# Linear attention with a GELU feed-forward on one core: weights loaded as fp32 pieces over two hardware queues in place of casting loads on GpSimd's queue

## The chip, the cores and the metric

The kernel runs on 1 core of one Trainium2 chip. The metric is the device time of one execution in microseconds, as a median of runs. The core has five engines: TensorE (PE, matmuls), VectorE (DVE), ScalarE (ACT), GpSimd (POOL) and SyncE (SP, here only for issuing DMAs). DMAs can be issued from SyncE's, ScalarE's and GpSimd's queues.

## What is computed

Linear attention with a decay per head (4 batches, 8 heads, 768 positions, head size 64), and on its output a feed-forward layer with the tanh form of GELU (512 to 2048 to 512 columns, 3072 rows, fp32 in and out):

```
for t in range(S):
    state = gamma[None, :, None, None] * state + np.einsum('bhd,bhe->bhde', k[:, :, t], v[:, :, t])
    y[:, :, t] = scale * np.einsum('bhd,bhde->bhe', q[:, :, t], state)
...
x = np.ascontiguousarray(attn_out.transpose(0, 2, 1, 3)).reshape(B * S, H * D)
h = x @ w_in
g = 0.5 * h * (1.0 + np.tanh(c * (h + 0.044715 * h * h * h)))
return (g @ w_out).astype(np.float32)
```

## The kernel before, in words

The 768 positions are cut into six chunks c of 128, and each chunk has the four batches b. What is done is a list of small steps, written out by hand in one string, `ORDER`. A word such as `PREP:q,0,2,P@1` calls the function `PREP` with chunk 0, batch 2 and engine P (A is ScalarE, V VectorE, P GpSimd, S SyncE); the numbers behind `@` name the buffers that the new tiles take. Every engine runs its own steps in the order of the list, and waits for what they need. So the list sets the order on each engine and in each DMA queue.

The steps of a chunk are these. `L` loads the rows of q, k or v of one batch as fp32, 256 KB, into one of 13 row buffers (class `r32`, slots 0 to 12). `PREP` converts them to fp16, and for some scales them by the decay. `T` with `ET`, or `DT` (a transposing DMA, from chunk 2 on), turns q and k. `A` and `EA` make the masked products of q and k, `SS` and `ES` the state, `YP` and `YI` the output of attention, and `EY` or `EP` bring it to SBUF as x, the input of the feed-forward layer.

The feed-forward layer has four blocks j of w_in (512 columns each) and of w_out (512 rows each). In most places its products are made by a scheme with seven products where eight would be plain: `M1` (seven for a chunk and a block) and `M2` (seven for the second product), with sums of weights made beforehand (`WI`, `WO`) and sums of inputs (`SX`, `SG`); `CP` and `D1` bring the results together, `G` is GELU. `HB` and `GB` are the plain form for one block and one batch of chunk 0: 16 matmuls with 128 columns against 4 matmuls with 256 columns in each `M1`. `O0` is the plain second product of chunk 0. `CO`, `D2` and `ST` (`ST0` for chunk 0) finish and store.

In the kernel before, block 1 of chunk 0 goes by `HB`, the other three by `M1`. The weights come by `LWI` (two DMAs for each block of w_in, one for each half of the partitions) and `LWO` (one for each block of w_out). These are issued on GpSimd and convert from fp32 to fp16 on the way; 23 of the 72 `L` are issued on GpSimd too. `SPIN` keeps TensorE running on zeros at the start. `HOLD` is a DMA of two fp16 numbers from a block of weights to a scratch tile, five of them on SyncE's queue; since it reads the weights, what follows it on SyncE's queue waits for them.

Of the kernel before, what the change touches and what calls it, by code (L numbers as in the profile page):

```python
# [31 lines left out]
GB:1,2,0@7 HB:1,1@5 ES:0,0,A GB:1,2,1@8 GB:1,0,1@9 PREP:q,1,2,V@2 PREP:k,1,2,V M1:0,3,3 HB:1,3@7 L:k,2,2,P@3
CP:0,3,12,A@1 GB:1,1,0 GB:1,1,1 T:1,1@6 L:q,2,1,P@4 ET:1,1,A@4 L:k,2,0,P@5 M1:0,3,7 T:1,3@0 L:v,2,0,P@12
T:1,2@3 D1:0,3,22 D1:0,3,12 O0:1,0@5 ET:1,3,A@5 ET:1,2,V@6 D1:0,2,22 M1:0,3,4 GB:1,3,1 L:q,2,0,P@0 T:1,0@6
WI:2,4,V GB:1,3,0 G:0,3,21@10 A:1,2@2,0 ET:1,0,A@0 EA:1,2,0@0 A:1,1@3,7 EA:1,1,1@1 O0:0,0@4 G:0,2,22@11 O0:1,1
A:1,3@6,2 EA:1,2,1 PREP:v,1,3,A@5 EA:1,1,0 A:1,0@7,0 M1:0,2,4 O0:0,1 PREP:v,1,1,A@6 G:0,2,21@12 EA:1,3,0@2
EA:1,0,1@3 EA:1,0,0 HOLD:1,2 YP:1,0@3,1 YP:1,1@6,0 PREP:v,1,0,A@7 YI:1,2 SS:1,2@7 L:v,2,3,P@9 EA:1,3,1 YI:1,0
L:q,2,2,S@11 WI:1,1,V WO:1,1,V G:0,3,11@13 YI:1,1 YI:1,3 EP:1,0,0,A@1 EP:1,0,1,V EP:1,1,0,A L:v,3,2,S@10
SS:1,1@2 SS:1,3 SS:1,0 G:0,3,12@14 O0:1,2 EP:1,1,1,A WO:2,1,V ES:1,1,V M1:1,0,1@3 M1:1,3,1@1 M1:1,1,2@6
G:0,3,22@15 CP:1,3,11,A@0 M1:1,1,1@0 SX:1,1,V@4 SX:1,3,V@5 CP:1,1,11,A@3 CP:1,0,11,A@1 WO:2,2,V SX:1,2,P@0  # L40
WI:1,3,V M1:1,3,2@7 O0:0,2 PREP:k,2,3,P@0 D1:1,3,11 O0:0,3 M1:1,1,5@7 G:1,3,11@16 ES:1,0,V EO:0,V@0 M1:1,3,5@2
PREP:k,2,1,A@2 M1:1,3,6 M1:1,0,2@4 CP:1,3,22,A@2 D1:1,1,11 WO:0,1,P G:1,1,11@17 PREP:q,2,3,P SX:1,4,P@1 O0:1,3
DT:2,3@1 CP:1,1,22,V@0 WO:3,1,P D1:1,0,11 PREP:k,2,2,A@3 L:v,2,1,S@6 M1:1,0,6 O0:2,0@6 CP:1,3,12,V@3
PREP:q,2,2,P PREP:v,2,2,P@0 M1:1,0,5@4 PREP:k,2,0,A@4 G:1,0,11@18 M1:1,3,7 M1:1,3,3 PREP:q,2,1,A CP:1,0,12,A@1
WI:1,2,V O0:2,1 PREP:q,2,0,P DT:2,1@2 DT:2,2@3 D1:1,3,22 LD:S D1:1,3,12 M1:1,1,6 EO:1,A@1 DT:2,0@0 HOLD:1,3
M1:1,1,3 L:v,3,3,S@1 WO:3,2,P G:1,3,22@19 CP:1,1,12,A@2 M1:1,0,7 WI:1,4,P G:1,3,12@20 M1:1,3,4 D1:1,1,12
G:1,3,21@21 A:2,3@2,5 M1:1,1,7 M1:1,2,5@7 O0:2,2 M1:1,2,1@1 EA:2,3,1@0 CP:1,0,22,A@3 PREP:v,2,1,P@3 D1:1,0,22
D1:1,1,22 WO:1,2,P G:1,1,12@22 G:1,1,22@23 EA:2,3,0 M1:1,0,3 L:k,3,0,S@2 M1:1,0,4 D1:1,0,12 O0:2,3
CP:1,2,22,V@2 CP:1,2,11,A@0 L:k,3,2,S@8 L:v,3,0,S@3 G:1,0,21@24 M1:1,1,4 M1:1,2,6 L:q,3,3,S@11 A:2,1@5,2
G:1,1,21@25 PREP:v,3,2,P@2 A:2,2@4,3 L:q,4,1,S@7 EO:2,V@2 EA:2,1,0@3 EA:2,2,1@1 G:1,0,22@26 A:2,0@0,6  # L50
CP:1,2,12,A@3 G:1,0,12@27 PREP:v,2,0,P@1 WO:0,2,P EA:2,0,0@2 L:q,3,2,S@5 PREP:v,2,3,P@4 M1:1,2,3 O0:3,0@5
O0:3,1 EA:2,0,1 L:q,3,0,S@4 M1:1,2,7 PREP:k,3,0,A@1 EA:2,1,1 YP:2,0@3,0 EA:2,2,0 L:k,3,3,S@0 L:k,5,1,S@6
YP:2,1@6,2 D1:1,2,12 YI:2,0 SG:1,1,1,P@28 L:q,3,1,S@10 PREP:v,3,3,P@6 L:q,4,2,S@12 SG:1,3,1,P@29 YI:2,1 YI:2,2
HOLD:0,0 YI:2,3 EP:2,0,1,V@0 SS:2,0@4 SS:2,3@7 D1:1,2,22 SS:2,2 EP:2,0,0,V SS:2,1 SG:1,1,2,P@30 ES:2,1,V
PREP:k,3,2,A@4 L:k,3,1,S@9 O0:3,2 G:1,2,22@31 M1:1,2,4 M1:1,2,2@0 EP:2,1,1,V O0:3,3 M1:2,0,1@3 D1:1,2,11
WO:0,3,P HOLD:0,3 WO:3,3,P ST0:2,S PREP:q,3,2,P L:v,3,1,S@2 PREP:q,3,3,A@0 M2:1,1,0,0@7 EP:2,1,0,V
# [10 lines left out]
M1:2,1,6 G:2,3,22@8 D1:2,1,11 PREP:v,3,1,P@5 G:2,3,12@11 A:3,0@5,3 A:3,2@2,0 PREP:v,3,0,P@7 L:k,4,1,S@9
SG:2,0,3,P@12 SG:1,1,3,P@10 CP:2,1,12,A@0 M1:2,1,3 M2:1,3,0,1 M2:1,6,0,0 WO:3,4,V EA:3,2,0@2 M1:2,2,1@2
M2:1,6,0,1 M2:1,3,1,0 M1:2,1,7 CO:1,12,A@2 M2:1,3,1,1 SG:1,3,3,P@15 EA:3,0,0@3 D1:2,1,12 EA:3,0,1 EA:3,2,1
D1:2,1,22 A:3,3@5,1 A:3,1@3,0 M1:2,1,4 L:q,4,3,S@0 G:2,1,21@24 EA:3,3,0@1 EA:3,3,1 EA:3,1,1@0 EA:3,1,0  # L70
L:v,5,2,S@12 CP:2,2,11,A@2 M2:1,7,1,0 M2:1,7,1,1 L:k,4,2,S@2 M2:1,7,0,0 PREP:v,4,0,P@1 D2:1,12, ST0:0,S
# [620 lines left out]
```

## Time and profile before

| what | value |
| --- | --- |
| median of 3 runs | 200.41 us (200.15 to 200.44) |
| the profiled execution's own time | 200.09 us |
| its span, first to last instruction | 198.3 us |
| mean granted TensorE clock | 0.98 |
| PE busy | 183.0 us (92%) |
| VectorE, ScalarE, GpSimd busy | 160.0, 119.3, 139.1 us |
| read from HBM, written | 27.63 MB, 6.29 MB |

The span leaves out what lies around the program's instructions, here 1.8 us. All times of the parts are from the one profiled execution. A busy share is an average over the whole span; which engine or transfer holds the others up differs from stage to stage. In rows of instructions, the numbers ahead are the start and the length in us, or the busy time and the mean in ns; `SPq` or `ACTq` is the sequencer of that engine when it issues a DMA.

### The profile page before, as it was taken

To read this page: it belongs to the slowest core of one execution; us is meant where nothing else is said; L and a number is where in the kernel's file an instruction comes from. 1 tells how busy PE (TensorE), PEld (TensorE's weight loads), DVE (VectorE), ACT (ScalarE), POOL (GpSimd) and SP (SyncE) were. 2 spreads that over 40 slices of the span, in tenths; PEclk is the share of its full clock that TensorE was granted. 3 is DMA by queue.
4 is the path that set the end of the run, shared out by engine and by line. 5 is a ranking of instruction groups with operands and counts; after the bars stand their busy time and mean duration, and the time that the engine had idled before them with its cause. 6 is when DMAs were issued, how large, how long until landed. Compare 5 with 4: busy or idle time off the path is not lost.

```text
span 198.3 us, 5294 instructions
## 1 busy us (share of the span) xinstructions
PE 183.0 (92%) x2111; PEld 149.0 (75%) x2111; DVE 160.0 (81%) x294; ACT 119.3 (60%) x219; POOL 139.1 (70%) x143
## 2 busy tenths in 40 slices
...
DMA  6999999999989999999999995260200201301453
GB/s 144 288 239 243 203 334 234 295 239 333 270 195 235 214 211 258 213 212 216 244 226 190 209 178 155 53 150 27 94 0 0 86 23 58 106 0 56 141 201 136
DMA packets 80540, 34.26 MB, mean 173 GB/s; under 512 B 69060, under 2 KB 78404, under 8 KB 80516
## 3 DMA queue, kind: packets, MB, share of 16 engines
q1 hardware_dynamic: 66164, 19.35, 44.4%
...
q10 hardware_dynamic: 8224, 4.36, 7.6%
...
HBM read 27.63 MB, written 6.29 MB: 171 GB/s over the span
## 4 chain that ended last, share of the span: by engine, by line
PE 65%; DMA 19%; POOL 6%; DVE 4%; issue 2%; ACT 1%; ACTq 0%; SPq 0%; POOLq 0%; DVEq 0%
PE bank L219 65%; DMA w_in<-in_moe_w_in_dram 9%; DMA r<-in_q_dram 6%; DMA qkT<-qk 2%; DVE g L216 2%; DMA r<-in_v_dram 2%; POOL sx L216 2%; POOL t_out L216 1%; POOL qk L216 1%; POOL v L216 1%; DVE h L216 1%; DVE w_out L216 1%; POOL g L216 1%; POOL w_in L262 0%; POOL qk L213 0%
## 5 line engine op out<-in xcount | busy, mean ns | idle before, releaser
L219 PEld LDWEIGHTS <-g 128*128 128x128 f16 x624 | 60.4, 98 | 11.8 <-PE bank L338 0.3
L216 POOL TENSOR_TENSOR g<-g 128x512 f16<-128x512 f16 x46 | 54.5, 1204 | 17.9 <-DVE g L216 7.2
L219 PE MATMUL bank<-w_out,g 128*128 128x256 f16 (+1 forms) x384 | 60.4, 290 | 0.2 <-DMA w_out<-in_moe_w_out_dram 0.2
L216 DVE TENSOR_TENSOR h<-bank,h 128x512 f32<-128x512 f32 x69 | 46.0, 682 | 8.8 <-PE bank L219 4.4
L442 ACT ACTIVATE g<-h 128x512 f16<-128x512 f32 x69 | 42.7, 634 | 15.4 <-DVE h L216 15.0
L219 PEld LDWEIGHTS <-w_in 128*128 128x128 f16 x432 | 39.2, 98 | 6.2 <-issue 0.8
L211 ACT COPY h<-bank 128x512 f32<-128x512 f32 x57 | 32.7, 588 | 13.0 <-PE bank L219 12.6
L219 PEld LDWEIGHTS <-t_in 128*128 128x128 f16 x276 | 26.4, 98 | 9.9 <-issue 4.3
L219 PE MATMUL bank<-t_out,g 128*128 128x256 f16 x240 | 33.4, 273 | 0.0
L216 DVE TENSOR_TENSOR a<-bank,mask 128x512 f16<-128x512 f32 x48 | 30.0, 680 | 3.5 <-PE bank L219 3.4
L219 PE MATMUL bank<-x,w_in 128*128 128x256 f16 (+1 forms) x248 | 29.7, 259 | 0.4 <-DMA w_in<-in_moe_w_in_dram 0.2
L219 PE MATMUL bank<-sx,t_in 128*128 128x256 f16 x184 | 26.5, 273 | 2.3 <-ACT g L442 1.2
L219 PE MATMUL bank<-sx,w_in 128*128 128x256 f16 x184 | 26.7, 273 | 0.0
L216 DVE TENSOR_TENSOR g<-g 128x512 f16<-128x512 f16 x34 | 22.1, 669 | 3.1 <-ACT g L442 2.1
L442 ACT ACTIVATE g<-bank 128x512 f16<-128x512 f32 (+1 forms) x31 | 16.5, 549 | 8.4 <-PE bank L219 5.8
L211 ACT COPY o<-bank 128x512 f32<-128x512 f32 (+1 forms) x19 | 9.7, 516 | 18.2 <-PE bank L219 18.2
L216 POOL TENSOR_TENSOR v<-r,cst 128x512 f16<-128x512 f32 x16 | 16.9, 1061 | 4.0 <-DMA r<-in_v_dram 4.0
L216 DVE TENSOR_TENSOR o<-bank,o 128x512 f32<-128x512 f32 (+1 forms) x18 | 10.6, 595 | 8.9 <-PE bank L219 8.7
L211 ACT CAST qk<-r 128x512 f16<-128x512 f32 x20 | 12.1, 620 | 6.2 <-PE bank L219 2.2
L219 PE MATMUL bank<-x,t_in 128*128 128x256 f16 x92 | 13.8, 273 | 1.9 <-DVE h L216 1.9
L216 DVE TENSOR_TENSOR qk<-r,cst 128x512 f16<-128x512 f32 x13 | 9.2, 744 | 6.5 <-DMA cst<-rr_cst 4.1
L211 ACT COPY qkT<-bank 128x1024 f16<-128x1024 f16 x7 | 6.9, 1013 | 8.0 <-PE bank L338 8.0
...
## 6 DMA issues: line engine op xcount, KB each, us to landing
r<-in_v_dram SPq DMA_DIRECT2D x15, 256.0 KB, 4.8
r<-in_q_dram SPq DMA_DIRECT2D x15, 256.0 KB, 4.2
r<-in_k_dram SPq DMA_DIRECT2D x14, 256.0 KB, 4.6
out_dram<-o ACTq DMA_DIRECT2D x11, 256.0 KB, 3.8
r<-in_v_dram POOLq DMA_DIRECT2D x9, 256.0 KB, 8.3
out_dram<-o SPq DMA_DIRECT2D x9, 256.0 KB, 2.3
w_in<-in_moe_w_in_dram POOLq DMA_DIRECT2D x8, 256.0 KB, 9.6
r<-in_k_dram POOLq DMA_DIRECT2D x8, 256.0 KB, 8.6
```

Of the source, the lines that this page charges most:

```text
L211: nc.scalar.copy(out=out, in_=in_)
L216: EN[e].tensor_tensor(out=out, in0=in0, in1=in1, op=op)
L219: nc.tensor.matmul(out=out, lhsT=lhsT, rhs=rhs, start=start, stop=stop, skip_group_check=True)
L442: nc.scalar.activation(out=out, in_=in_, func=AF.Gelu_apprx_tanh, scale=1.0)
```

## The change

The weights no longer come by converting DMAs from GpSimd. Each block of w_in and of w_out is loaded in four pieces of 128 rows and 512 columns as fp32 (for w_in the 128 rows are two runs of 64, 256 rows apart) (`WLI`, `WLO`, 256 KB each, 32 in all) into the row buffers that `L` uses, over SyncE's queue (26 pieces) and ScalarE's (6). A piece is then converted into its place in the fp16 block by `CWLI` or `CWLO`, 14 of them on ScalarE and 18 on GpSimd. All 72 `L` go over SyncE's (33) and ScalarE's (39) queues. The five `HOLD` are gone. Block 0 of chunk 0 now goes by `HB` too, so four `HB` and eight `GB` take the place of seven `M1`, three `CP`, three `D1` and four `G`. `ORDER` is written anew as a whole; some steps change their engine (`SG` on GpSimd 46 to 52, `PREP` on GpSimd 34 to 42, `CP` on VectorE 12 to 19). The new functions:

```diff
+    def WLI(j, kc, e):
+
+        t = new("r32", ("wi32", j, kc), [128, 512], F32)
+        src = moe_w_in.rearrange("(u k p) n -> u p k n", u=2, p=64)[:, :, kc, j * 512:(j + 1) * 512]
+        EN[e].dma_start(out=t, in_=src)
+
+    def WLO(j, kc, e):
+        t = new("r32", ("wo32", j, kc), [128, d_model], F32)
+        fc = 4 * j + kc
+        EN[e].dma_start(out=t, in_=moe_w_out[fc * 128:(fc + 1) * 128])
+
+    def CWLI(j, kc, e):
+        copy_on(e, w_in[j][:, kc], tiles["wi32", j, kc])
+
+    def CWLO(j, kc, e):
+        copy_on(e, w_out[j][:, kc], tiles["wo32", j, kc])
```

The beginning of the old and of the new order, up to where the first products of w_out begin in the new one:

```diff
-L:k,0,2,A@0 L:q,0,2,A@1 ZERO L:k,0,0,S@2 SPIN:11@0 LI:A L:q,0,3,A@3 LC:S TABLE PREP:k,0,0,V@0 L:k,0,3,A@4
-L:q,0,1,A@5 L:v,0,1,S@6 PREP:q,0,2,P@1 LWI:0 PREP:k,0,2,V L:v,0,3,P@7 MASK L:k,0,1,S@8 L:q,0,0,S@9
-PREP:q,0,3,V@2 T:0,2@1 ET:0,2,A@0 A:0,2@2,3 L:v,0,0,P@10 PREP:k,0,3,V LWI:2 L:v,0,2,S@11 T:0,3@4 PREP:q,0,0,V
-ET:0,3,A@1 PREP:k,0,1,P@3 EA:0,2,1@0 A:0,3@5,6 T:0,0@7 EA:0,2,0 ET:0,0,A@2 PREP:q,0,1,V T:0,1@0 LWI:3
-A:0,0@1,4 PREP:v,0,2,P@0 EA:0,3,0@1 EA:0,3,1 EA:0,0,0@2 EA:0,0,1 ET:0,1,A@3 LWI:1 SS:0,2@3 A:0,1@2,7
-EA:0,1,0@3 PREP:v,0,0,P@1 PREP:v,0,1,A@2 PREP:v,0,3,A@3 YI:0,2@5 SS:0,1@6 L:k,1,1,P@12 EA:0,1,1 EY:0,2,A@0
-L:q,1,3,S@2 YI:0,3@1 L:q,1,1,P@1 YI:0,0@4 WI:0,1,V L:q,1,2,P@0 WI:0,2,V SS:0,3 YI:0,1@0 EY:0,3,A SX:0,1,V@0
-EY:0,0,A EY:0,1,A L:k,1,0,P@3 SS:0,0 WI:0,3,V M1:0,0,5@2 M1:0,0,1@7 WI:0,4,V SX:0,2,V@1 SX:0,3,V@2
-CP:0,0,11,A@0 L:k,1,3,P@4 SX:0,4,V@3 L:k,1,2,P@9 M1:0,0,2@5 M1:0,2,1@1 LWO:0 M1:0,0,6 WI:2,1,V CP:0,0,22,A@1
-CP:0,2,11,A@2 D1:0,0,11 M1:0,2,2@4 WI:2,3,V M1:0,2,5@0 M1:0,0,3 CP:0,0,12,A@3 L:q,1,0,P@8 LWO:1 WI:2,2,V
-L:v,1,2,P@5 D1:0,2,11 G:0,0,11@0 CP:0,2,22,A@0 D1:0,0,12 M1:0,0,7 M1:0,2,6 G:0,2,11@1 ES:0,1,A L:v,1,3,P@11
-G:0,0,12@2 D1:0,0,22 L:v,1,1,P@10 L:v,1,0,P@6 M1:0,2,3 M1:0,3,2@5 WI:3,1,V CP:0,2,12,A@2 M1:0,0,4 M1:0,3,1@4
-PREP:q,1,3,V@4 WI:3,3,V LWO:2 PREP:q,1,0,P@1 LWO:3 D1:0,2,12 L:v,2,2,P@7 WI:3,2,V CP:0,3,11,A@3 M1:0,3,5@2
-L:k,2,1,P@2 G:0,2,12@3 PREP:q,1,1,V@3 D1:0,3,11 L:q,2,3,P@8 WI:3,4,V M1:0,2,7 G:0,0,21@4 HB:1,0@3 PREP:k,1,0,V
...
+WLI:1,3,A@0 ZERO L:k,0,2,S@1 SPIN:11@0 LC:S L:q,0,3,S@2 L:k,0,1,A@3 PREP:k,0,1,V@0 L:k,0,3,S@4 MASK
+L:q,0,1,A@5 PREP:q,0,1,V LI:A PREP:k,0,3,V@1 L:q,0,2,A@6 L:k,0,0,S@7 PREP:k,0,2,V@2 L:v,0,3,A@8 L:q,0,0,A@9
+T:0,1@1 L:v,0,1,A@10 WLI:0,3,A@11 PREP:q,0,3,P TABLE T:0,3@2 L:v,0,2,S@12 PREP:q,0,2,V CWLI:1,3,P ET:0,3,V@0
+L:k,1,1,S@3 WLI:2,2,A@5 T:0,2@3 ET:0,2,V@1 PREP:v,0,3,P@0 PREP:q,0,0,V@3 A:0,2@4,5 PREP:k,0,0,P ET:0,1,A@2
+A:0,3@6,7 T:0,0@0 EA:0,2,1@0 L:v,0,0,S@4 WLI:0,2,S@1 EA:0,3,0@1 A:0,1@2,3 WLI:2,1,A@2 EA:0,3,1 ET:0,0,A@3
+PREP:v,0,2,A@1 WLI:0,0,S@6 CWLI:2,2,P YI:0,3@1 PREP:v,0,1,P@2 PREP:v,0,0,P@3 EY:0,3,A@0 A:0,0@5,6 EA:0,1,0@2
+EA:0,2,0 PREP:k,1,1,P@4 EA:0,1,1 CWLI:2,1,A SS:0,3@7 WLI:0,1,S@0 CWLI:0,2,A WLI:2,0,S@8 YI:0,2@0 EA:0,0,1@3
+WLI:2,3,S@9 SS:0,2 YI:0,1@1 EA:0,0,0 YI:0,0@2 WLI:3,0,S@7 CWLI:0,1,P SS:0,0@4 CWLI:2,0,P CWLI:0,3,A CWLI:0,0,A
+WLI:3,1,S@12 EY:0,1,A EY:0,0,V EY:0,2,V SS:0,1 WI:2,1,V HB:0,3@3 WLI:1,2,S@5 WLI:3,3,S@10 ES:0,1,A CWLI:2,3,A
+WLI:3,2,S@4 SX:0,1,V@0 HB:0,1@6 CWLI:3,0,A GB:0,3,1@0 WI:0,1,V L:k,1,0,A@3 GB:0,3,0@1 M1:0,2,1@5 L:q,1,0,A@2
+WLI:1,1,S@1 ES:0,0,A WI:2,2,V CWLI:3,1,P M1:0,2,5@1 HB:0,2@2 M1:0,2,2@0 SX:0,2,V@1 CP:0,2,11,V@0 M1:0,3,1@7
+WI:3,1,V WLI:1,0,S@0 HB:0,0@3 CWLI:3,3,P L:k,1,2,S@8 GB:0,2,0 SX:0,4,V@2 CWLI:1,0,P CWLI:3,2,A GB:0,1,0@2
+L:q,1,2,S@11 CP:0,2,22,V@1 CWLI:1,1,P GB:0,2,1 L:q,1,1,S@6 CP:0,3,11,A@2 L:v,1,0,A@9 M1:0,3,5@4 CWLI:1,2,A
+SX:0,3,V@3 WI:2,3,V M1:0,3,2@2 L:q,1,3,S@7 WI:3,3,V PREP:q,1,2,P@1 M1:0,2,6 PREP:q,1,1,P WI:3,2,V L:k,2,2,A@12
+D1:0,2,11 WI:2,4,P M1:0,2,3 D1:0,3,11 L:k,1,3,S@10 G:0,2,11@3 WI:3,4,V CP:0,2,12,A@3 PREP:q,1,3,P@2 G:0,3,11@4
+GB:0,1,1@5 HB:1,0@0 L:v,1,2,A@0 PREP:k,1,2,V L:v,1,3,S@4 WI:1,1,V HB:1,1@2 PREP:k,1,0,V@3 PREP:q,1,0,V
+M1:0,3,6 CP:0,3,22,A@0 HB:1,3@6 M1:0,2,7 GB:0,0,1 GB:1,1,1@6 PREP:k,1,3,P M1:0,3,3 WLO:0,3,S@1 PREP:v,1,0,P@4
+L:v,1,1,A@5 D1:0,2,12 GB:1,0,0@7 GB:1,0,1 T:1,2@1 WLO:0,1,S@11 WLO:0,2,S@6 WLO:1,0,S@7 GB:1,1,0 CP:0,3,12,V@2
+M1:0,3,7 GB:0,0,0 ET:1,2,A@4 D1:0,2,22 PREP:v,1,1,P@5 WLO:0,0,S@8 T:1,1@0 T:1,0@2 A:1,2@3,1 GB:1,3,1@8
+D1:0,3,12 D1:0,3,22 ET:1,1,V@5 PREP:v,1,2,P@6 ET:1,0,A@6 EA:1,2,1@1 WLO:1,3,S@3 M1:0,2,4 M1:0,3,4 G:0,2,21@9
+PREP:v,1,3,P@7 A:1,1@4,0 G:0,3,12@10 EA:1,2,0 G:0,3,21@11 A:1,0@2,1 T:1,3@5 EA:1,1,0@0 EA:1,0,1@2 EA:1,0,0
+HB:1,2@3 ET:1,3,A@1 GB:1,3,0@12 YP:1,0@7,4 EA:1,1,1 WLO:1,1,S@2 A:1,3@1,2 CWLO:0,1,P EA:1,3,0@3 YI:1,0 YI:1,1
+G:0,2,12@13 YP:1,1@5,6 L:q,2,1,A@10 WLO:2,1,S@9 SS:1,1@0 SS:1,0 YI:1,2 EA:1,3,1 CWLO:0,3,P EP:1,0,1,A@1
+ES:1,0,V EP:1,0,0,A SS:1,3@1 SS:1,2 G:0,2,22@14 YI:1,3 WLO:2,0,S@5 M1:1,0,2@2 M1:1,3,1@4 EP:1,1,1,A CWLO:0,2,P
+WLO:1,2,S@0 ES:1,1,V GB:1,2,0 M1:1,1,1@0 M1:1,0,1@7 EP:1,1,0,A CP:1,0,11,A@2 WLO:3,2,S@4 PREP:k,2,2,P@0
+CWLO:0,0,P WI:0,2,V L:q,2,0,A@11 SX:1,1,V@4 M1:1,3,2@6 SX:1,3,V@5 CWLO:2,1,P G:0,3,22@15 CP:1,3,11,A@3
+O0:0,0@1 WLO:2,2,S@1 D1:1,0,11 GB:1,2,1 O0:2,0@5 CP:1,1,11,V@1 CWLO:1,1,A M1:1,1,2@2 D1:1,3,11 SX:1,2,P@0
+CWLO:1,2,A CWLO:2,0,A L:q,2,2,S@6 M1:1,3,5@3 CWLO:1,0,P WLO:2,3,A@12 CWLO:1,3,P G:1,0,11@16 SX:1,4,P@1
+M1:1,0,6 D1:1,1,11 L:k,2,1,A@8 M1:1,3,6 G:1,3,11@17 WI:0,4,V M1:1,0,5@6 O0:1,0@2 WI:1,2,V PREP:q,2,1,P@4
...
```

More of the change, by code (lines that the diff above doesn't have):

```diff
@@ L32 @@
[L32 to L56, printed above, removed]
@@ L67 @@
[L67 to L71, printed above, removed]
@@ L92 @@
-SG:2,3,4,V@14 M2:2,5,0,0@6 G:3,3,22@13 HOLD:1,1 M1:3,2,5@5 CP:3,2,12,A@2 EP:4,1,0,V SG:3,3,1,P@24 M1:4,1,1@4
-ES:4,0,V G:3,3,12@28 ST0:3,A CP:3,2,22,A@3 M2:2,7,0,0 SG:3,1,2,P@9 PREP:q,5,3,A@1 M2:2,5,1,0 M2:2,7,1,0
-M1:3,2,3 SG:2,2,3,P@36 M2:2,5,1,1 M1:4,1,2@0 M1:3,2,7 M1:4,0,1@1 PREP:k,5,0,A D1:3,2,12 M1:3,2,2@2 M2:2,5,0,1
-SX:4,1,V@0 D1:3,2,22 M1:4,1,5@5 CP:4,1,11,V@0 SX:4,2,P@4 M1:4,1,6 G:3,2,12@25 D1:4,1,11 L:v,5,3,S@9 D1:3,2,11
-M2:2,7,1,1 G:3,2,22@4 SX:4,4,P@3 CP:4,1,22,V@2 M1:4,0,2@0 CO:2,22,A@4 SX:4,3,P@1 DT:5,0@0 PREP:q,5,2,P@3
@@ new lines @@
+G:1,3,22@19 PREP:k,2,1,P WO:3,1,V D1:1,3,12 L:v,2,0,A@1 PREP:q,2,0,P@3 G:1,3,12@20 D1:1,0,12 M1:1,1,5@3
+CP:1,1,12,V@2 PREP:q,2,2,A M1:1,3,4 CWLO:3,1,A M1:1,2,1@6 M1:1,1,7 D1:1,0,22 CWLO:3,3,P O0:1,2 G:1,3,21@21
+M1:1,0,4 WO:1,2,P WI:1,4,V CP:1,1,22,A@0 O0:2,3 L:k,2,0,S@12 DT:2,1@0 PREP:q,2,3,P@2 DT:2,2@2 M1:1,1,3
+D1:1,1,22 G:1,0,22@22 G:1,0,21@23 L:v,2,1,A@4 O0:1,3 G:1,0,12@24 M1:1,1,4 PREP:k,2,0,A O0:0,2 PREP:k,2,3,A
+G:1,1,21@25 WO:2,2,P CP:1,2,11,A@1 D1:1,1,12 SG:1,0,1,P@26 DT:2,0@3 M1:1,2,5@4 M1:1,2,2@7 DT:2,3@5 WO:0,2,P
@@ new lines @@
+G:2,3,22@21 CP:2,0,12,A@0 M1:2,1,7 M2:1,5,1,0 D1:2,1,22 DT:3,0@4 SG:1,3,2,V@4 SG:1,2,4,P@10 M1:2,3,3
+M2:1,5,1,1 M2:1,6,1,0 M2:1,5,0,1 M2:1,6,0,0 DT:3,3@0 L:q,5,1,S@3 SG:1,0,3,V@0 G:2,1,22@1 M1:2,3,4
+PREP:v,3,0,P@7 M1:2,1,3 WO:3,2,V WO:2,4,P M1:2,1,4 CO:1,22,A@5 PREP:q,4,2,P SG:1,3,4,P@8 CP:2,0,22,A@3
+G:2,3,21@12 D1:2,3,12 M1:2,0,7 L:q,4,1,A@4 WO:1,4,P WO:0,3,P D1:2,1,12 G:2,1,21@9 M2:1,3,1,0 D1:2,0,22
+M1:2,0,3 M2:1,6,0,1 A:3,1@4,5 L:k,5,3,A@6 A:3,2@7,2 ST0:1,S D1:2,0,12 EA:3,1,1@1 EA:3,2,0@0 M1:2,0,4
```

157 lines of the change are left out of this document (86 added, 71 removed).

## The prediction

> **What bounds the kernel now.** I read the busy table and the slices first, then the chain of waits, then the list of DMA issues.
>
> ```profile
> span 198.3 us, 5294 instructions
> PE 183.0 (92%) x2111; PEld 149.0 (75%) x2111; DVE 160.0 (81%) x294; ACT 119.3 (60%) x219; POOL 139.1 (70%) x143
> ...
> DMA  6999999999989999999999995260200201301453
> GB/s 144 288 239 243 203 334 234 295 239 333 270 195 235 214 211 258 213 212 216 244 226 190 209 178 155 53 150 27 94 0 0 86 23 58 106 0 56 141 201 136
> ```
>
> PE (TensorE) works 183.0 of 198.3 us, so the kernel is PE's; the DMA engines are full for the first 24 of 40 slices (about 120 us). The chain shows where both meet:
>
> ```profile
> 8.16 7.23 DMA w_in<-in_moe_w_in_dram
> ...
> 15.67 11.33 DMA w_in<-in_moe_w_in_dram
> ...
> 110.71 84.05 PE bank L219 x924
> ```
>
> Until 27.0 us the path is the loading of w_in; from 110.7 on it is matmuls without a pause. So the question for any change of the loads is when w_in is complete on chip, and how much PE work comes after that.
>
> **How an issue is spread over the DMA engines.** This decides the forecast. The packets of the two hardware queues, and the issues on them:
>
> ```profile
> q1 hardware_dynamic: 66164, 19.35, 44.4%
> ...
> q10 hardware_dynamic: 8224, 4.36, 7.6%
> ...
> r<-in_v_dram SPq DMA_DIRECT2D x15, 256.0 KB, 4.8
> r<-in_q_dram SPq DMA_DIRECT2D x15, 256.0 KB, 4.2
> r<-in_k_dram SPq DMA_DIRECT2D x14, 256.0 KB, 4.6
> out_dram<-o ACTq DMA_DIRECT2D x11, 256.0 KB, 3.8
> ...
> out_dram<-o SPq DMA_DIRECT2D x9, 256.0 KB, 2.3
> ...
> out_dram<-o SPq DMA_DIRECT2D x7, 128.0 KB, 1.7
> r<-in_q_dram ACTq DMA_DIRECT2D x3, 256.0 KB, 5.1
> r<-in_k_dram ACTq DMA_DIRECT2D x2, 256.0 KB, 4.2
> qkT<-qk SPq DMA_TRANSPOSE x16, 3.7
> dec<-rr_dec SPq DMA_DIRECT2D x1, 256.0 KB, 3.5
> out_dram<-o ACTq DMA_DIRECT2D x1, 128.0 KB
> cst<-rr_cst SPq DMA_DIRECT2D x1, 74.0 KB
> misc<-w_out SPq DMA_DIRECT2D x3, 0.0 KB
> iden<-rr_ident ACTq DMA_DIRECT2D x1, 32.0 KB
> misc<-w_in SPq DMA_DIRECT2D x2, 0.0 KB
> ```
>
> ScalarE's queue, q10: 5 row tiles of 128 x 8 runs are 5120 packets, iden 128, nine ST of 128 x 2 runs 2304, two ST0 256, the half store 128: 7936. The other 288 are 18 issues times 16: each issue has one closing packet on each of 16 engines. SyncE's queue, q1: 44 row tiles 45056, 16 transposes 16384, cst and dec 256, seven ST and two ST0 2048, seven halves 896, and 16 closing packets for each of the 62 plain copies, 992: 65632. That leaves 532 for the 16 transposes' closings and the five HOLD (the misc rows). Whatever whole number a transpose closes with, its part divides by 16, so the HOLDs' part is 4 over a multiple of 16; their 5H does that for H = 4 (with 32 per transpose), and not for 3 (one engine: two elements, one closing) nor for 18 (sixteen). A HOLD's pattern is one row of two elements. So it went over two engines, an element and a closing packet on each: an issue is cut along the outermost count above one, 128 for all others and 2 here.
>
> The new WLI reads its piece of w_in as [2, 64, 512] (u outermost) into [128, 512]. Cut along the outermost counts of both sides it can go over 2 engines only. The trace has no issue whose two sides differ, so both ends stay open: 2 or 16 engines. I take 2, by the HOLD, the only row with an outer 2.
>
> The Trainium skill, "DMA: Bandwidth & Descriptors", section "Why a DMA increments its semaphore by 16 and not by 1", states the mixed case: the largest number up to 16 that divides both outer counts. By that rule it is 2, and the sum below stands; cut into 16 parts it would be the first rival's 199 us. No row here shows the mixed case.
>
> **Part by part.** The rates, clock and window rows:
>
> ```profile
> 22.00:24.00 2.00, 2.00 (x21) 1.79 (x19) 2.00 (x5) 1.97 (x5) 0.53 (x1) 1.00 1.24 203
> ...
> 5.00:7.00 2.00, 1.06 (x3) 0.15 (x1) 1.78 (x3) 0.73 (x2) 0.66 (x1) 1.00 1.28 288
> ...
> 0.00:2.50 2.50, 1.31 (x4) 1.00 0.11 25
> 2.50:5.00 2.50, 2.50 (x7) 1.00 1.14 266
> 27.10:198.30 171.20, 162.83 (x1908) 1.00 0.68 163
> 54.00:84.00 30.00, 29.71 (x341) 1.00 1.00 221
> ...
> 10.00:15.00 5.00, 3.81 (x39) 2.65 (x36) 4.28 (x8) 1.60 (x2) 5.00 (x8) 0.50 1.25 243
> ```
>
> *WLI, 16 pieces.* On two engines each carries 64 rows of 2 KB per piece, 131,072 bytes. At 22 to 24 us only weights move: 203 GB/s written as fp16 is 406 GB/s read, 25.4 per engine, so 5.2 us a piece and 82.6 us for 16, if every piece takes the same two engines. This is the big term.
>
> *The row tiles on the same two engines.* SyncE's order puts 12 weight pieces, WLI:1,0 the last, ahead of L:k,1,2 and what follows. Ahead of or beside that piece the two queues carry the 12 tiles of chunk 0, k,1,1, and on ScalarE's queue k,1,0, q,1,0 and up to two more: 17 tiles, 16 KB of each on each engine. Two hardware queues together moved 288 GB/s (18 per engine): 0.91 us a tile, 15.5 us. SyncE's queue alone, at 54 to 84 us, moved 221. The Trainium skill, "DMA: Bandwidth & Descriptors", section "Issuing engines are not separate DMA queues", says that issuing from several engines adds no bandwidth. By it the tiles would go at 221: 20.2 us, and the sum would be 280; the trace, 288 against 221, speaks against it.
>
> *Start.* 25 GB/s in the first 2.5 us against 266 in the next puts the first packets at 2.3 us. The last piece of w_in is on chip at 2.3 + 82.6 + 15.5 = 100.4 us.
>
> *Conversion.* CWLI on GpSimd is a cast like this one, 0.63 us:
>
> ```profile
> L213 POOL CAST v<-r 128x512 f16<-128x512 f32 x3 | 1.9, 632 | 0.9 <-DMA r<-in_v_dram 0.9
> L308 POOL DMA_DIRECT2D r<-in_v_dram x9 | 8.0, 904 | 1.8 <-DMA r<-in_v_dram 1.8
> ```
>
> With 1 us from last packet to waiter (an estimate; a 128 KB store, 0.6 us at 221 GB/s, landed 1.7 us after issue), HB:1,0, which needs all of w_in[1], starts at 102.0. The other 31 conversions (0.63 us each) lie in the wait for later pieces or behind PE work. One holds more than itself: CWLI:2,2 stands on GpSimd ahead of PREP:v,0,1 and PREP:v,0,0, so chunk 0's last YI wait for the third or fourth piece; HB:0,3 behind them waits for the seventh anyway.
>
> *PE.* HB (16 matmuls) and M1 (4):
>
> ```profile
> 25.04 0.60 PE L219 MATMUL bank<-x,t_in 128*128 128x256 f16 x4
> 25.48 0.60 PE L219 MATMUL bank<-x,w_in 128*128 128x256 f16 x4
> ...
> 27.14 1.95 PE L219 MATMUL bank<-x,w_in 128*128 128x128 f16 x32 [0.18 <-DMA w_in<-in_moe_w_in_dram]
> ...
> 31.02 1.06 PE L219 MATMUL bank<-x,w_in 128*128 128x128 f16 x16
> 31.91 0.61 PE L338 MATMUL bank<-iden,qk 128*128 128x128 f16 x8
> ```
>
> An M1 takes 0.44 us start to start, an HB 0.89. For chunk 0 and j = 0 four HB (3.56) replace seven M1 (3.05): +0.5. Ahead of HB:1,0 stood 16 M1 (7.0 us), now four HB and eight M1 (7.1), so +0.4 falls behind it. Before, the first HB:1 (27.1 us) had 171.2 us to the end; now 171.6.
>
> *What lies behind the last piece.* SyncE's queue then brings k,1,2 and four tiles (0.91 each), then w_out pieces, whose both sides have 128 outermost: 0.65 us each at 406 GB/s. T:1,2 comes after three HB and three M1, 4.0 us; k,1,2 needs 0.9 + 1 + a PREP. O0:0,0 stands 13 us of PE work after HB:1,0; w_out[0] is complete after five tiles and five pieces, 7.8 us, plus a cast. Covered; without that cover, at most these 7.8 us.
>
> *Off the path.* GpSimd loses 23 row issues at 0.9 us and the casting loads; ScalarE issues 45 loads that it must get past before its next copy, but through the first 100 us it waits for pieces. HOLD's waits go. Beside an 80 us wait these cost nothing; with that cover gone they are in the first rival.
>
> *Waits of PE behind HB:1,0.* Of the old 171.2 us PE worked 162.83; 3.5 of the 8.4 idle are the tail, so at most 4.9 can go, since rows now come over two queues. Against that, PE restarts after a long idle: at 10 to 15 us, after its first pause, the granted clock was 0.50, and 5 us at half clock cost 2.5. I count the two as even; bounds -5 and +6.
>
> Sum: 102.0 + 171.6 = 273.6 us of span. The profiled execution took 200.09 for its 198.3, so 275.4, and the median of three, 200.41, stands 0.3 above: 275.7, said as 276.
>
> **Rivals.**
> First, the other side: the pieces go over all 16 engines. Then a piece costs 0.65 us, w_in is there by about the time it was, and the rows' 288 in place of 221 GB/s and GpSimd's freed queue can end waits: 4.9 at most after 27 us, say 3.3; PE's +0.5 and a later first transpose (iden is now ScalarE's fourth issue, MASK stands ahead of PREP:q,0,1; +1.5) take most back: 200.4 - 1.3 = 199.1. It holds if pieces land within about 3 us of each other's issue. Against it: the HOLD. Chance 0.05.
> Second, the pieces take different pairs, so the two queues' pieces run side by side: half of 82.6, 234. For it: nothing shows which engines a HOLD took. Chance 0.04.
> Third, two engines, but 2 KB rows go no faster than single-queue row tiles (221 / 16 = 13.8 GB/s): 152 us for the pieces and 20 for the tiles, 350. Against it: 25.4 was seen. Chance 0.03.
>
> **Numbers.** The forecast has 0.88. Its own range: pieces at 26.2 GB/s (share 1.28 in place of 1.24) to 21 (slice six, 334): 80 to 100 us; tiles hidden beside pieces, -15.5, or not; waits -5 to +6. Not all at once: 256 to 297 holds nine tenths of it, 0.8 of all. About 0.2% is what a measurement of this kernel can tell from no change. Of the first rival 0.03 is faster and 0.01 the same; the rest is slower: 0.96.
>
> **What would show it.** The first HB:0 near 52 us (2.3, seven pieces 36.1, 13 tiles 11.8, 1.6 to convert); PE idle some 80 us before HB:1,0, waiting for w_in's copies; pieces landing 5 us apart; DMA share under 3 tenths in most slices from 20 to 100 us; a q1 count of 57992 packets (12 pieces closing with 2), where 16 engines would give 58160. Wrong if pieces land within 3 us, or if HB:1,0 starts before 85 us.

## The result, and the profile after

The changed kernel takes 277.51 us (median of 4, 276.44 to 280.2) against 200.43 us (median of 4, 200.15 to 201.61) for the kernel before: ratio 1.3851, 95% interval 1.3737 to 1.3965. The profiled execution took 276.44 us for a span of 274.3. The forecast was 276. Times here and below are medians of all executions of a kernel; the ratios leave out the few that fell into a slower state of the chip, one each of e1_split, e7_lwi and e12_less among them.

The profile page of the changed kernel, the lines that answer to those of before (busy time, slices, the first queue):

```profile
span 274.3 us, 5420 instructions
PE 195.3 (71%) x2147; PEld 158.1 (58%) x2147; DVE 166.5 (61%) x299; ACT 116.0 (42%) x217; POOL 131.0 (48%) x135
...
PE   7071202371310339999999898999999999899995
...
PEclk9755555557555557999999999999999999999999
DMA  6881111112121379999999999987366300021235
GB/s 164 196 195 51 53 51 51 51 51 72 61 86 50 102 186 264 343 311 258 191 269 278 199 223 246 245 176 164 86 160 110 117 31 11 1 79 38 96 117 174
...
q1 hardware_dynamic: 57992, 23.02, 33.9%
```

From the fourth slice to the thirteenth the DMA engines are busy for one or two tenths and move 50 to 86 GB/s; PE does little, most of it at half clock. Behind that, from 103 us on, the picture is that of the kernel before. PE's busy time is 12.3 us longer, 8.5 of it ahead of HB:1,0 and 3.8 behind it; the forecast had 0.5 for the changed products, and most of the rest is half clock.

A window inside the idle part (the columns after the engines are granted clock, DMA share, GB/s), and what each queue moved in it (packets, MB, share of 16 engines):

```profile
30.00:40.00 10.00, 0.00 (x0) 0.00 (x0) 0.00 (x0) 0.00 (x0) 0.12 (x1) 0.50 0.13 51
```

```profile
q1 hardware_dynamic: 128, 0.26, 6.6%
q10 hardware_dynamic: 126, 0.25, 6.5%
```

A share of 0.13 is 2 of 16 engines, full. Without the closing packets these are 250 packets of 2 KB in 10 us, 25.6 GB/s for each of the two. Both queues had pieces here and took turns packet for packet, 128 and 126, on the same two engines.

The timeline of SyncE's issues, of PE and of GpSimd (start, duration; in brackets the wait before it and its releaser):

```profile
15.78 69.76 SPq L281 DMA_DIRECT2D r<-in_moe_w_in_dram  x12
```

```profile
52.35 3.60 PE L224 MATMUL bank<-x,w_in 128*128 128x128 f16 x32 [9.62 <-ACT w_in L216]
...
100.14 0.29 PE L224 MATMUL bank<-x,w_in 128*128 128x128 f16 x1 [7.32 <-POOL w_in L218]
```

```profile
39.88 0.61 POOL L218 CAST w_in<-r 128x512 f16<-128x512 f32 x1 [21.45 <-DMA r<-in_moe_w_in_dram]
...
99.47 1.17 POOL L218 CAST w_in<-r 128x512 f16<-128x512 f32 x2 [15.78 <-DMA r<-in_moe_w_in_dram]
```

SyncE needs 69.8 us to issue its 12 pieces. It waits for no more than 0.03 us between them: the issues themselves last up to 10 us each. The first HB starts at 52.35, the last piece is converted from 99.47 on, and HB:1,0 starts at 100.14. Of the 274.3 us, 174.2 lie behind it.

PE's waits (total us, times, longest) name the conversions first, then what was queued behind them:

```profile
PE bank L224 <- ACT w_in L216: 15.5, 3, 9.6
PE bank L224 <- POOL w_in L218: 13.6, 4, 7.3
PE bank L224 <- POOL v L218: 12.0, 1, 12.0
PE bank L224 <- ACT g L464: 10.3, 1, 10.3
PE bank L360 <- DVE qk L221: 8.5, 1, 8.5
```

The 12.0 us for v are CWLI:2,2: at 39.88 on GpSimd, ahead of PREP:v,0,1. The 8.5 us for qk are rows of chunk 0 that stand behind the first piece, WLI:1,3, on ScalarE's queue.

### The profile page after: what moved, and what is told of

The parts are those of the page before. It is cut to its first block, busy times and chain, and to the rows that moved or that the text cites. A ratio compares the mean times of both kernels' runs of the same rounds, so it can differ in the third digit from the quotient of the medians.

```text
span 274.3 us, 5420 instructions
## 1 busy us (share of the span) xinstructions
PE 195.3 (71%) x2147; PEld 158.1 (58%) x2147; DVE 166.5 (61%) x299; ACT 116.0 (42%) x217; POOL 131.0 (48%) x135
## 3 DMA queue, kind: packets, MB, share of 16 engines
q1 hardware_dynamic: 57992, 23.02, 33.9%
## 5 line engine op out<-in xcount | busy, mean ns | idle before, releaser
L224 PEld LDWEIGHTS <-w_in 128*128 128x128 f16 x480 | 46.9, 110 | 50.6 <-ACT w_in L216 26.5
L221 POOL TENSOR_TENSOR g<-g 128x512 f16<-128x512 f16 x52 | 61.0, 1191 | 19.8 <-ACT g L464 11.5
L224 PE MATMUL bank<-x,w_in 128*128 128x256 f16 (+1 forms) x304 | 39.5, 288 | 39.6 <-ACT w_in L216 15.5
L224 PE MATMUL bank<-w_out,g 128*128 128x256 f16 (+1 forms) x384 | 56.8, 290 | 0.0
L221 DVE TENSOR_TENSOR h<-bank,h 128x512 f32<-128x512 f32 x66 | 43.3, 681 | 8.1 <-PE bank L224 4.9
L218 POOL CAST w_in<-r 128x512 f16<-128x512 f32 x8 | 5.3, 671 | 75.9 <-DMA r<-in_moe_w_in_dram 75.9
L216 ACT COPY h<-bank 128x512 f32<-128x512 f32 x47 | 26.8, 585 | 24.5 <-PE bank L224 16.0
L224 PE MATMUL bank<-t_out,g 128*128 128x256 f16 x240 | 32.1, 273 | 0.0
L216 ACT CAST w_in<-r 128x512 f16<-128x512 f32 x8 | 4.6, 615 | 48.1 <-DMA r<-in_moe_w_in_dram 48.1
L221 DVE TENSOR_TENSOR qk<-r,cst 128x512 f16<-128x512 f32 x9 | 6.1, 707 | 19.4 <-DMA r<-in_k_dram 19.4
L224 PE MATMUL bank<-a,v 128*64 128x128 f16 x192 | 9.2, 237 | 12.1 <-POOL v L218 12.0
```

What stands on the lines that cost most here:

```text
L216: nc.scalar.copy(out=out, in_=in_)
L218: EN[e].tensor_copy(out=out, in_=in_)
L221: EN[e].tensor_tensor(out=out, in0=in0, in1=in1, op=op)
L224: nc.tensor.matmul(out=out, lhsT=lhsT, rhs=rhs, start=start, stop=stop, skip_group_check=True)
```

## The experiments

The theory: a piece goes over as many DMA engines as divide the outermost counts of both its sides, 2 here, and that alone is the loss. Its rivals: something else in the pieces (their width, conversions, order), or costs beside them. This table puts the runs together; starts are from the traces, each of one execution, "rest" is the span behind the start of HB:1,0, "(one)" is a single run. Ratios are to runs of the kernel before beside each (medians 199.7 to 202.1).

| kernel | time, us | ratio to before, 95% | HB:1,0 at | rest |
|---|---|---|---|---|
| before | 200.4 | 1 | 27.1 | 171.2 |
| changed | 277.5 | 1.385 (1.374 to 1.397) | 100.1 | 174.2 |
| e1_split | 212.9 | 1.061 (1.056 to 1.067) | 39.6 | 171.4 |
| e2_cols | 283.4 (one) | | 105.6 | 175.9 |
| e4_u4 | 240.9 (one) | | 59.6 | 179.3 |
| e4_u8 | 223.8 (one) | | 42.2 | 179.5 |
| e4_u16 | 212.3 | 1.056 (1.049 to 1.064) | 36.0 | 174.3 |
| e5_oneq | 225.7 (one) | | 42.2 | 181.7 |
| e6_before_nopool | 213.5 | 1.062 (1.054 to 1.070) | 35.4 | 175.2 |
| e7_lwi | 212.0 | 1.052 (1.044 to 1.061) | 39.2 | 174.2 |
| e8_cast | 212.2 | 1.053 (1.044 to 1.062) | 34.3 | 175.9 |
| e10_both | 213.0 | 1.055 (1.047 to 1.062) | 32.5 | 177.4 |
| e11_e1both | 212.1 | 1.053 (1.045 to 1.061) | 37.5 | 172.0 |
| e12_less | 209.9 | 1.051 (1.042 to 1.060) | 29.3 | 176.2 |

**The number of engines.** First the piece in two issues, by halves of the partitions, each with 64 outermost:

```diff
-        EN[e].dma_start(out=t, in_=src)
+        for u in range(2):
+            EN[e].dma_start(out=t[u * 64:(u + 1) * 64], in_=src[u])
```

> Each piece of w_in is loaded by two issues, one per half of the partitions ([64, 512] on both sides), all else as in the changed kernel. Theory 1 (an issue is cut along the outermost counts of both sides, so [2, 64, 512] into [128, 512] uses two engines): both sides now have 64 outermost, so 16 engines; 16 pieces cost 10.3 us at 406 GB/s instead of 82.6, with 17 row tiles (15.5 us at 288 GB/s) and the start (2.3) the last piece is there at 28 us, HB:1,0 starts near 30, and with 174 us behind it the span is about 204 us, less if waits go: 199 to 206. Rival A (an fp32 piece costs about 5 us by its rows, or because a queue works on one issue at a time): over 260 us, as now. Rival B (the conversions and the new order make the waits, not the loads): over 250 us.

212.9 us: of 77 us lost, 64.6 come back. That is less than expected: the span is 211.0, not 199 to 206, and HB:1,0 comes at 39.6, not near 30. Then two issues again, but by columns, so that the outermost counts stay 2 and 128:

```diff
+        for u in range(2):
+            EN[e].dma_start(out=t[:, u * 256:(u + 1) * 256], in_=src[:, :, u * 256:(u + 1) * 256])
```

> Each piece of w_in is loaded by two issues, cut by columns: [2, 64, 256] into [128, 256] each. As many issues as in the split by partitions, but the outermost count of the source stays 2. Theory 1: still two engines, now with 1 KB rows, the same bytes: 276 us or, where shorter rows are dearer, up to 300; 51 GB/s or less while only pieces move. Rival A in its form that one issue is slow and two run side by side: about 235 us.

283.4 us, and the same window as above reads

```profile
30.00:40.00 10.00, 0.00 (x0) 0.00 (x0) 0.57 (x1) 0.00 (x0) 0.00 (x0) 0.50 0.14 48
```

So it isn't the number of issues that helps, but what is outermost in each. Then one issue per piece with 4, 8 and 16 outermost (`u=2, p=64` becomes `u=4, p=32`, `u=8, p=16`, `u=16, p=8`):

> The 512 rows of w_in are read in another order, [4, 32, 512] into [128, 512] for each piece in one issue: the same bytes, issues and row length, only the outermost count of the source is 4 (the rows then do not belong to the inputs they are multiplied with, which leaves the work as it is). Theory 1: four engines; pieces 41.3 us, tiles 15.5, start 2.3, HB:1,0 near 61 us, span 61 + 174 = 235 (228 to 242), 102 GB/s while only pieces move. Rivals A and B: 274 us as before.

> As the kernel with four runs of rows, but [8, 16, 512] into [128, 512]. Theory 1: eight engines; pieces 20.6 us, HB:1,0 near 40 us, span about 214 (206 to 220), 203 GB/s while only pieces move. Rivals A and B: 274 us.

> The source of WLI read as [16, 8, 512] in place of [2, 64, 512], still one issue per piece; the rows of w_in then come in another order, so this part of the computation is changed. If an issue goes over as many engines as the outermost count, 16 here, this is the split piece (212.9 us) with half the issues on SyncE: 12 of about 0.5 us go away there. Theory 1 (the rest of the loss of the split kernel is issue time on SyncE's and ScalarE's queues in the first 40 us): HB:1,0 moves from 39.6 to 33 to 36 us, the time to 204 to 208 us. Rival (the rest is the new order of rows and masks at the start and the half clock there, or the bandwidth of the queues): HB:1,0 stays near 39.6, the time within 1% of 212.9.

A window of each while pieces arrive, in this order:

```profile
25.00:35.00 10.00, 1.62 (x32) 1.33 (x32) 1.29 (x2) 0.00 (x0) 3.29 (x5) 0.50 0.26 102
```

```profile
20.00:26.00 6.00, 0.60 (x10) 0.44 (x12) 0.75 (x2) 0.00 (x0) 1.82 (x4) 0.50 0.54 207
```

```profile
18.00:26.00 8.00, 3.06 (x64) 2.59 (x64) 2.82 (x5) 1.96 (x4) 3.90 (x6) 1.00 1.06 300
```

Shares of 0.26, 0.54 and 1.06 are 4, 8 and 16 engines; 51, 102 and 207 GB/s are 25.6, 25.5 and 25.9 per engine. The count of engines is shown. The kernel with 8 missed its range all the same (a span of 221.8 for 206 to 220): HB:1,0 came near the expected 40, but 179.5 us lay behind it, not 174. The same runs follow the rule for the mixed case that the prediction took from the Trainium skill ("DMA: Bandwidth & Descriptors", section "Why a DMA increments its semaphore by 16 and not by 1"): 2, 4, 8 and 16 against 128.

**What is left: 12 us.** With 16 engines the kernel is still 6% slower than before, where the prediction's first rival had said 199.1. The split kernel's trace offered SyncE's issue time, 24 half pieces, and ScalarE's, which issues loads until it comes to its first own work at 15.12:

```profile
12.38 21.97 SPq L282 DMA_DIRECT2D r<-in_moe_w_in_dram  x24
```

```profile
12.60 2.49 ACTq L282 DMA_DIRECT2D r<-in_moe_w_in_dram  x2
15.12 1.28 ACT L241 ACT_TABLE_LOAD   x1 [15.12 <-DMA r<-in_q_dram]
...
18.60 1.01 ACT L216 COPY qkT<-bank 128x1024 f16<-128x1024 f16 x1 [1.99 <-DMA r<-in_moe_w_in_dram]
```

The run with 16 outermost halves the issues. HB:1,0 comes 3.6 us earlier (36.0, as the theory of issue time had it), the time stays (212.3, as its rival had it).

Half clock is a part that no run here takes out alone. The row of this kernel above gives a granted clock of 1.00 from 18 to 26 us, but its clock records begin only at 30.8, and its first 32 matmuls with w_in take as long as the same 32 at a clock of 0.50 in the changed kernel (3.60 at 52.35); in the kernel before, at 1.00, they took 1.95 (27.14):

```profile
27.27 3.60 PE L224 MATMUL bank<-x,w_in 128*128 128x128 f16 x32 [6.17 <-ACT w_in L216]
```

What half clock adds to PE's own work is inside PE's busy time, 186.6 us here and 183.0 before. So of the 12 us it can be 3.6 at most in this way, and the other 8.4 are waits.

All loads on SyncE's queue (ScalarE's loads become SyncE's in the order, nothing else):

```diff
-WLI:1,3,A@0 ZERO L:k,0,2,S@1 SPIN:11@0 LC:S L:q,0,3,S@2 L:k,0,1,A@3 ...
+WLI:1,3,S@0 ZERO L:k,0,2,S@1 SPIN:11@0 LC:S L:q,0,3,S@2 L:k,0,1,S@3 ...
```

> The kernel with split pieces, but with every load on SyncE's queue. If ScalarE's own loads hold back its first copies (ET:0,1 and A:0 waited for it by 15 to 21 us) and the second queue brings nothing, the first transposes and A come earlier and the time is at or below 212.9. If the second queue carries bandwidth (288 against 221 GB/s) and issue time, the pieces come later: 24 + 8 half pieces and 17 rows at some 0.5 us each on one engine end near 42 to 48 us, HB:1,0 there, time 215 to 223.

225.7 us, 12.8 more than with two queues. From 5 to 10 us, while only row tiles move, first this kernel and then the split one:

```profile
5.00:10.00 5.00, 0.98 (x3) 0.15 (x1) 1.58 (x5) 0.00 (x0) 2.06 (x2) 0.92 1.00 227
```

```profile
5.00:10.00 5.00, 0.33 (x2) 0.00 (x0) 1.64 (x6) 0.00 (x0) 2.14 (x2) 0.79 1.26 285
```

A second queue carries bandwidth. HB:1,0 was expected here at 42 to 48 and came at 42.2, but the rest grew by 10 us. No single wait of PE in it is longer than 3.1, and its time is 2.7 above the expected 223. This is one run.

Two kernels without fp32 pieces for w_in. The kernel before, with only GpSimd's 23 row loads put on SyncE:

```diff
-PREP:q,0,3,V@2 T:0,2@1 ET:0,2,A@0 A:0,2@2,3 L:v,0,0,P@10 ...
+PREP:q,0,3,V@2 T:0,2@1 ET:0,2,A@0 A:0,2@2,3 L:v,0,0,S@10 ...
```

> The kernel before with GpSimd's 23 row loads put on SyncE's queue at the same places, nothing else. If GpSimd's issue time (0.9 us each) is off the path, as the forecast took it, the time is the same within 0.7%, 199 to 202 us. If SyncE's single queue makes rows late, slower, 202 to 206. If GpSimd's issues held up its copies on the path, faster, 195 to 199.

213.5 us: slower, as the second expectation had it, but by 13 us in place of at most 6, and by as much as all that is left. Its queues from 14 to 20 us, and the first conversion of v on GpSimd, which stood at 14.08 us in the kernel before:

```profile
q0 software_dynamic: 965, 0.93, 91.3%
q1 hardware_dynamic: 963, 0.24, 30.3%
```

```profile
22.94 0.61 POOL L213 CAST v<-r 128x512 f16<-128x512 f32 x1 [9.93 <-DMA r<-in_v_dram]
```

The casting load of w_in and the rows take turns packet for packet, 965 and 963, and a row's packet is 256 bytes: rows get 0.24 MB in 6 us, 41 GB/s. In the kernel before, GpSimd's rows v,0,3 and v,0,0 stood in the casting loads' own queue, ahead of the later ones, and SyncE's queue was that much shorter. The kernel before shares packets in the same way (877 and 874 in this window); the difference is that its rows of v had gone ahead. So that queue did ordering work. The other kernel takes the changed order and its row loads, but the old casting loads for w_in:

```diff
...
+        first = {(2, 2): 2, (0, 2): 3, (2, 1): 1}
+        if (j, kc) in first:
+            LWI(first[j, kc])
...
+        if (j, kc) == (1, 3):
+            LWI(0)
```

> The changed kernel with its order and its row loads, but w_in by the old casting loads on GpSimd's queue (LWI:0 to LWI:3, no fp32 pieces and no CWLI for w_in; w_out stays as fp32 pieces). Theory 1 (the whole loss lies before HB:1,0 and comes from the pieces of w_in): HB:1,0 at 27 to 31 us, 171 to 172 us behind it, time 200 to 205 us. Rival (rows on ScalarE's queue, w_out's pieces, their 16 conversions or the new order cost time of their own): more than 174 us behind HB:1,0, time above 206.

212.0 us, so the rival is right: fp32 pieces over 16 engines and casting loads cost the same in this order. Its trace, and its starts in the table, are of an execution of 215.53 us; PE's longest wait in it is again for a row of v beside casting loads:

```profile
PE bank L224 <- POOL v L218: 10.8, 1, 10.8
```

**Can the 12 us be ordered away?** In the kernel with 16 outermost PE waited 6.2 us for ScalarE's conversions. On ScalarE, CWLI:2,1 waited for its piece, with three conversions that HB:0,3 needs queued behind it, while GpSimd had already converted a later piece at 21.73:

```profile
25.03 2.18 ACT L216 CAST w_in<-r 128x512 f16<-128x512 f32 x4 [6.04 <-DMA r<-in_moe_w_in_dram]
```

```profile
21.73 0.62 POOL L218 CAST w_in<-r 128x512 f16<-128x512 f32 x1 [0.26 <-DMA r<-in_moe_w_in_dram]
```

```diff
-EA:0,2,0 PREP:k,1,1,P@4 EA:0,1,1 CWLI:2,1,A SS:0,3@7 ...
+EA:0,2,0 PREP:k,1,1,P@4 EA:0,1,1 SS:0,3@7 ...
-... CWLI:0,3,A CWLI:0,0,A
+... CWLI:0,3,A CWLI:0,0,A CWLI:2,1,A
```

> The kernel with the source read as [16, 8, 512] (rows of w_in in another order, so that part of the computation is changed), and CWLI:2,1 moved on ScalarE from ahead of CWLI:0,2, CWLI:0,3 and CWLI:0,0 to behind them. There HB:0,3 waited 6.2 us for ScalarE's conversions, whose first, CWLI:2,1, started only at 25.0, while CWLI:2,0, of a later piece than all of w_in[0], had started at 21.7. Theory 2 (what is left of the loss with 16 engines is the order of the conversions on ScalarE): HB:0,3 at 22 to 24 us in place of 27.3, HB:1,0 at 32 to 33 in place of 36.0, time 207.5 to 209.5. Rival (the pieces themselves or the rows behind them come too late, so the wait only moves): HB:0,3 earlier, but T:1,2 stays at 42 to 43, time 211 to 213.

HB:0,3 starts at 22.3 in place of 27.3, as expected; HB:1,0 at 34.3 in place of 36.0, less than expected; the time is the same, 212.2. Of 4.9 us, 1.7 are left at HB:1,0 and nothing at M1:1,0,2 (50.87 against 50.88). T:1,2, which the rival had staying at 42 to 43, came at 39.6, so the loss moved to behind it. With the start rearranged too (iden first, MASK and WLI:1,3 later), on one issue with 16 outermost and on the split pieces:

```diff
-WLI:1,3,A@0 ZERO L:k,0,2,S@1 ... L:k,0,3,S@4 MASK
-L:q,0,1,A@5 PREP:q,0,1,V LI:A PREP:k,0,3,V@1 ...
+LI:A ZERO L:k,0,2,S@1 ... L:k,0,3,S@4
+L:q,0,1,A@5 PREP:q,0,1,V PREP:k,0,3,V@1 MASK ...
+... L:v,0,1,A@10 WLI:1,3,A@0 WLI:0,3,A@11 ...
```

> The kernel with CWLI:2,1 moved (rows of w_in in another order as there), and the start rearranged too: iden first on ScalarE's queue, WLI:1,3 behind the rows of chunk 0 and its conversion beside CWLI:2,2, MASK behind PREP:k,0,3. Theory 2 (start and conversions both cost): T:0,1 at 8.0 to 8.5 us in place of 9.9, 1 to 2 us less than with CWLI:2,1 moved alone, 206 to 208. Rival (from 20 us on the pieces set the time): the same as with CWLI:2,1 moved alone, within 0.5 us.

> The kernel with split pieces (w_in in its own order), with both rearrangements, of the conversions and of the start. SyncE still issues 24 half pieces. Theory 2 with issue time on SyncE as a third term: HB:0,3 at 25 to 26 in place of 27.5, HB:1,0 at 37 to 39.6, time 209 to 212. If issue time is no term, as the kernel with the start rearranged and single issues, 206 to 208. Faster than the kernel before (200.4) by neither.

T:0,1 starts at 7.97, as expected, and HB:1,0 at 32.5; the time is 213.0, nearer to the rival (212.2 within 0.5) than to the theory's 206 to 208. On split pieces it is 212.1, where 209 to 212 was expected. Each wait that went was made up for further on: M1:1,0,2 starts at 50.9 with 16 outermost, at 50.9 with the conversion moved, at 52.1 with the start moved too. Two of these waits can be read in the trace of the kernel with both changes on single issues. A row of v is issued on ScalarE's queue at 40.05 and takes 8.4 us to land, while pieces of w_out arrive on SyncE's (the issue with its KB and the us to landing; then both queues from 40.6 to 43.4 and from 43.6 to 46):

```profile
r<-in_v_dram ACTq DMA_DIRECT2D x1, 256.0 KB, 8.4
```

```profile
q1 hardware_dynamic: 402, 0.74, 78.7%
...
q10 hardware_dynamic: 2, 0.00, 0.1%
```

```profile
q1 hardware_dynamic: 344, 0.63, 69.0%
q10 hardware_dynamic: 891, 0.23, 41.6%
```

For some 3 us behind its issue the row doesn't move at all, then it goes faster than the pieces. PE waits 2.1 us for it.

And ScalarE's stream, where a row load stands ahead of a copy; in brackets, what the copy's engine waited for before it:

```profile
37.35 0.37 ACTq L330 DMA_DIRECT2D r<-in_v_dram  x1
37.76 0.59 ACT L216 COPY h<-bank 128x512 f32<-128x512 f32 x1 [2.83 <-POOL qk L221]
```

The load L:v,1,2 can't go before 37.31; the copy behind it, which needs nothing of that, waits too, and PE waits 1.9 us for the copy. The bracket names GpSimd, but the load's buffer was free: GpSimd had converted the piece in it, WLI:1,0, by 32.1. What came at 37.28 was the landing of a row of q that SyncE had issued at 30.33. In the trace the loads of SyncE's and ScalarE's queues share eight semaphores that tell of landings, this row and L:v,1,2 the same one, and wherever the traces record the landings, no load starts before the last one with its semaphore has landed. So at most eight loads of these two queues are under way at a time. The issues of GpSimd in the kernel before have eight semaphores of their own. Taking the loads off GpSimd gave that up; what it costs, no run here tests.

The last run takes away traffic, with a constant from VectorE in place of what isn't loaded:

```diff
+        for j in (2, 3):
+            nc.vector.memset(w_in[j], 0.02)
...
+        if j > 1:
+            EN[e].dma_start(out=t[0:32], in_=src[:, 0:2])
+        else:
+            EN[e].dma_start(out=t, in_=src)
...
+        if j > 1:
+            copy_on(e, w_in[j][0:32, kc], tiles["wi32", j, kc][0:32])
```

> The kernel with both rearrangements and single issues, with a quarter of each of the eight pieces of w_in[2] and w_in[3] loaded and converted (32 of 128 partitions); the rest of these two is a constant set by VectorE in its idle first microseconds, so this part of the computation is changed. 1.57 MB are not loaded, 5.2 us at the 300 GB/s at which the pieces went; every instruction of the four engines stays, and so does their order. Theory 3 (what is left is load traffic: the DMA engines were full from 3 to 36 us, and the rows of chunk 1 stand behind the pieces): T:1,2 at 34 to 35.5 us in place of 38.8, time 207 to 209. Rival (ScalarE's, VectorE's and GpSimd's own work and order between 20 and 50 us sets the time): T:1,2 may move, but M1:1,0,2 stays at 50 to 52 us, time 211 to 213.

M1:1,0,2 starts at 46.8 in place of 52.1, which the rival excluded; T:1,2 at 36.95 in place of 38.83, which the theory had earlier still. The time, 209.9, is between the two, and the ratios (1.051 and 1.055) have intervals that overlap. That less traffic shortens the kernel isn't shown. Nor is it shown that the earlier starts come from traffic alone: they are from the fastest of four executions, 207.37 us, and it had its full clock back earlier. From 18 to 26 us, first the last kernel, then the one with both rearrangements:

```profile
18.00:26.00 8.00, 5.79 (x108) 4.93 (x103) 5.36 (x11) 5.95 (x14) 5.00 (x8) 1.00 0.73 202
```

```profile
18.00:26.00 8.00, 6.39 (x94) 5.65 (x93) 4.37 (x10) 5.39 (x11) 3.96 (x6) 0.50 1.06 302
```

The wait on ScalarE is there too, and grew, here with PE's wait for it:

```profile
35.45 0.39 ACTq L338 DMA_DIRECT2D r<-in_v_dram  x1
35.88 0.58 ACT L216 COPY h<-bank 128x512 f32<-128x512 f32 x1 [4.72 <-POOL qk L221]
```

```profile
PE bank L224 <- ACT h L216: 3.1, 1, 3.1
```

How the 12 us divide between traffic, the packet-for-packet sharing, the eight semaphores with the loads that block ScalarE, and half clock isn't settled. No kernel run here is faster than the kernel before.

## Why the prediction was right

- *Two engines.* Right, and shown from both sides. The count of 57992 packets on q1 was forecast to the packet; e2_cols and the three counts of outermost tell it from every other cause tried.
- *Size of the big term.* 25.4 GB/s per engine, taken from a casting load over 16 engines, against 25.6 measured over 2. With the row tiles at 0.91 us this gave the first HB near 52 (52.35) and HB:1,0 at 102.0 (100.14). The second rival (different pairs) falls with the window of 51 GB/s while both queues had pieces; the third (13.8 GB/s per engine) with its 25.6.
- *Two rates for the row tiles.* 276 by the trace's two-queue rate, 280 by the rule of the Trainium skill ("DMA: Bandwidth & Descriptors", section "Issuing engines are not separate DMA queues") that issuing from several engines adds no bandwidth, 277.5 measured: too near to part them. The run with one queue does: 227 against 285 GB/s while only row tiles move. The trace decides against the rule here. How much of that run's 12.8 us is bandwidth isn't shown.
- *Behind HB:1,0.* 171.6 forecast, 174.2 measured. Waits that would go and half clock had been counted even, up to 4.9 against 2.5. The windows behind HB:1,0, first the changed kernel, then the split one, at full clock there:

```profile
100.14:274.34 174.20, 166.59 (x1912) 0.98 0.69 168
```

```profile
39.64:211.02 171.38, 164.03 (x1912) 136.16 (x1912) 148.62 (x256) 101.08 (x190) 121.72 (x118) 1.00 0.71 171
```

  Half clock costs the 2.6 us between 166.6 and 164.0. PE's own work is 1.2 above the 162.8 of before, where the forecast had 0.4. The waits hardly went: PE is idle for 7.6 us, 8.4 before. So half clock was right and the gain was too large by far. The two misses, 1.9 early at HB:1,0 and 2.6 late behind it, nearly cancel; that the sum came within 1.5 of 277.5 is luck in this part.
- *Conversions.* 0.61 us each, behind their pieces, as said. CWLI:2,2 held GpSimd to 39.9, not to the third or fourth piece's time (about 30), and the first transposes came at 14.6, 6.5 later than before. Both lay within the wait for pieces, so they cost nothing here.
- *"Off the path ... these cost nothing; with that cover gone they are in the first rival."* Here the prediction was wrong, though nothing hung on it at a chance of 0.05. With 16 engines the time is 212 to 213, not 199.1. The failed term is the "4.9 at most, say 3.3" for waits that would go: it took row loads off GpSimd as a relief. e6_before_nopool shows that this move costs 13 us in the kernel before, where the casting loads stay, by rows that share engines packet for packet with them; how much of it carries over to the changed kernel isn't shown. Pieces over 16 engines were priced at 0.65 us (406 GB/s) and went at 300. And ScalarE's issues were priced at nothing; they held its copies by 2 to 5 us at a time.
